# A float64 guard as a scale of ACT's absolute value, and squares, a division and copies moved from DVE to ACT and POOL, in attention followed by a squared-ReLU feed-forward layer

## The chip, the core and the metric

The kernel runs on one core of one Trainium2 chip. The metric is the device time of one execution in microseconds (us); lower is better. The core has a matrix engine (PE, with its weight loads PEld), a vector engine (DVE), an activation engine (ACT) and a general engine (POOL), each with its own queue of instructions that it works through in order. SP issues most DMAs, in order too, and ACT issues some. The engines and the DMAs wait for one another through semaphores.

## The reference

Two parts, one after the other. An attention between `x` (8 batches, 8 heads, 512 rows, 64 wide) and `state` (8, 8, 32, 64), read in both directions:

```python
scores = scale * np.matmul(x, state.transpose(0, 1, 3, 2))
a = np.exp(scores - scores.max(-1, keepdims=True)); a /= a.sum(-1, keepdims=True) + 1e-09
xread = np.matmul(a, state)
scores2 = scale * np.matmul(state, x.transpose(0, 1, 3, 2))
...
sread = np.matmul(a2, x)
return np.concatenate([xread, sread], axis=2).astype(np.float32)
```

Its output, 4352 rows of 512, goes through a feed-forward layer with a squared ReLU; `w_in` (512 x 2048) and `w_out` (2048 x 512) arrive as float64:

```python
h = x @ w_in
r = np.maximum(h, 0.0)
g = r * r
return (g @ w_out).astype(np.float32)
```

## The kernel before

**Exact halves.** A float32 factor is cut into two parts of a shorter format, `hi` and `lo`, by `split` (L96 to L98): ACT copies the value into the short format (L97), and the engine passed as `eng_lo` subtracts that from the value (L98). A product is then three matrix products.

**The weights.** They come as words of 64 bits, read as two 32-bit words. `singles` (L100 to L120) turns one 128x512 tile of them into float32: ACT takes the absolute value of the upper word (L107), DVE bounds it from below (L108), shifts and masks its bits (L109), puts the sign in (L113) and the topmost bits of the lower word (L117). Sixteen tiles of `w_in` (`w_raw` to `wf`, in `convert` of `z_part`) and sixteen of `w_out` (`wo_raw` to `wof`, in `wo_load`) go through it. The raw tiles share four buffers with other loads (tag `raw`); SP issues a load when a buffer is free, which is when L117 has read the tile in it.

**z.** The attention's first output times `w_in` is not formed from the output: for each batch the state is multiplied by `w_in` first. `z_part(G, k, g)` does this for a group `G` of four batches, 256 columns `k` of `w_in` and half of the heads `g`: load, `convert`, `cut` (a `split`, left out in the first six parts), and two products, whose result ACT copies out (`z_stage`, L215) and sends to DRAM (`zd`, L217). `z_fetch(b, k)` loads the batch's share of it back (`z_raw`, L230) and splits it into `z_hi` and `z_lo`. `z_state(0)` loads and splits the state for this (`stz_hi`, `stz_lo`, L141).

**The attention.** For a batch `b` and each half of the heads: `scores`, then `soft1` and `soft1b` (probabilities over the state, giving `a_hi` and `a_lo`), and, some batches later, `turn` (the other direction's probabilities `e2`, divided by their sum at L338 to L340, and transposed) and `read`.

**The feed-forward.** `mlp` takes a batch's 512 rows through columns `fc` of the hidden layer, 128 at a time. One such step is called a unit: `up` makes `ph` from z and a (six matmuls, L392), ReLU on ACT (L394), the square (on ACT for the first ten units, L396, on DVE for all others, L398) and a `split` into `g_hi` and `g_lo`; `down`, two units later, adds twelve matmuls (L418) into four banks `po`. At the end of a part, `rows` empties the four banks: with `move`, which takes DVE and ACT in turn, or with an addition on DVE (L599) where the sum exists already. The batches 0 and 1 are taken in two parts each (`BOTH`, L67: units 0 to 5 of batch 0, units 0 to 9 of batch 1, and then the rest of both), since the weights come in during that time; from batch 2 on a batch is one part of 16 units. After the eight batches a last pass of 16 units takes the rows of the state's direction.

**What sets the order.** The program is written in an order that two lists of steps with due times (`Ahead`, L475) interleave with the units. The scheduler behind the program then orders each engine's instructions anew by a timeline that it simulates, so a change in one instruction moves others.

Of the kernel before, what the change touches and what calls it, by code (L numbers as in the profile page):

```python
# [9 lines left out]
F32 = mybir.dt.float32  # L10
F32R = mybir.dt.float32r
I32 = mybir.dt.int32
AF = mybir.ActivationFunctionType
# [5 lines left out]
def memory_attention_then_relu2_ffn(  # L19
# [22 lines left out]
    nc = tc.nc  # L42
# [10 lines left out]
    NFC = DF // P  # L53
# [42 lines left out]
    def split(hi, lo, src, eng_lo):  # L96
        nc.scalar.copy(out=hi, in_=src)  # L97
        eng_lo.tensor_sub(out=lo, in0=src, in1=hi.bitcast(F32))  # L98

    def singles(out_f, words):  # L100

        low, high = words[..., 0], words[..., 1]
        bits = out_f.bitcast(I32)
        nc.scalar.activation(out_f, high.bitcast(F32), AF.Abs)  # L107
        nc.vector.tensor_scalar_max(out_f, out_f, 2.0**-15)  # L108
        nc.vector.tensor_scalar(  # L109
            out=bits, in0=bits, scalar1=3, scalar2=0x3FFFFFF8,  # L110
            op0=ALU.logical_shift_left, op1=ALU.bitwise_and,
        )
        nc.vector.scalar_tensor_tensor(  # L113
            out=bits, in0=high, scalar=-0x40000000, in1=bits,
            op0=ALU.bitwise_and, op1=ALU.bitwise_or,
        )
        nc.vector.scalar_tensor_tensor(  # L117
            out=bits, in0=low, scalar=29, in1=bits,
            op0=ALU.logical_shift_right, op1=ALU.bitwise_or,
        )  # L120


    def z_state(G):
        if G == 0:
            raw = sb.tile([P, H, GB * N], F32, name="st_f", tag="x_hl", bufs=1)
            st["raw"] = raw
        else:
            raw = sb.tile([P, H, GB * N], F32, name="st_raw", tag="raw", bufs=RAW)
        for j in range(2):
            nc.sync.dma_start(out=raw[j * D:(j + 1) * D].rearrange("d h m -> d (h m)"), in_=stT[G])  # L130
        hi = sb.tile([P, H, GB * N], F32R, name="stz_hi", bufs=1)
        lo = sb.tile([P, H, GB * N], F32R, name="stz_lo", bufs=1)
        if G:
            split(hi, lo, raw, nc.gpsimd)
        else:
            for i in range(2):
                own = slice(i * D, (i + 1) * D)
                other = slice((1 - i) * D, (2 - i) * D)
                for v in (hi, lo):
                    nc.gpsimd.memset(v[other, i::2, :].bitcast(F32), 0.0)  # L140
                split(hi[own, i::2, :], lo[own, i::2, :], raw[own, i::2, :], nc.vector)  # L141
        st[G] = hi, lo

    def z_part(G, k, g):
# [111 lines left out]
    def attention_group(b, g, pair):  # L256
# [79 lines left out]
        def turn():  # L336
            s2 = my["s2"]
            nc.vector.tensor_scalar_add(s2, s2, EPS)  # L338
            nc.vector.reciprocal(s2, s2)
            nc.vector.tensor_scalar_mul(my["e2"], my["e2"], s2)  # L340
            pt = ps_x.tile([P, NT, P], F32, name="pt", tag="px")
            for t in range(NT):
                nc.tensor.transpose(  # L343
                    out=pt[:, t, :], in_=my["e2"][:, t * P:(t + 1) * P], identity=ident
                )
            hl = sb.tile([P, NT, NQ, 2, 2 * N], F32R, name="e_hl", bufs=1)
            src = pt.rearrange("p t (q n) -> p t q n", n=2 * N)
            split(hl[:, :, :, 0, :], hl[:, :, :, 1, :], src, nc.vector)
            my["e"] = hl
# [31 lines left out]
    def mlp(width, fcs, first, rows, aux):  # L381
# [6 lines left out]
        def up(fc):  # L388
            ph = ps_h.tile([P, S], F32, name="ph", tag="ph")[:, :width]
            todo = first(fc)  # L390
            for i, (w, v) in enumerate(todo):
                nc.tensor.matmul(ph, lhsT=w, rhs=v, start=i == 0, stop=i == len(todo) - 1)  # L392
            r = sb.tile([P, S], F32, name="r", bufs=2)[:, :width]
            nc.scalar.activation(r, ph, AF.Relu)  # L394
            if units[0] < 10:
                nc.scalar.activation(ph, r, AF.Square)  # L396
            else:
                nc.vector.tensor_mul(out=ph, in0=ph, in1=r)  # L398
            units[0] += 1
            hi = sb.tile([P, S], F32R, name="g_hi", bufs=2)[:, :width]  # L400
            lo = sb.tile([P, S], F32R, name="g_lo", bufs=2)[:, :width]
            split(hi, lo, ph, nc.vector)
            gs[fc] = hi, lo
# [28 lines left out]

    units = [0]

    def move(t, dst, po):
        if t % 2:
            nc.scalar.copy(out=dst, in_=po)
        else:
            nc.vector.tensor_copy(out=dst, in_=po)
# [135 lines left out]
    for b, fcs in parts:  # L575
# [17 lines left out]
        def rows(t, po, b=b, fcs=fcs):  # L593
            if fcs[0] == 0:
                if t == 0:
                    sums[b] = sb.tile([P, NT, DM], F32, name="sum", bufs=2)
                move(t, sums[b][:, t, :], po)
            else:
                nc.vector.tensor_add(out=sums[b][:, t, :], in0=sums[b][:, t, :], in1=po)  # L599
            if fcs[-1] == NFC - 1:  # L600
                nc.sync.dma_start(
                    out=out[b * R + t * P:b * R + (t + 1) * P, :], in_=sums[b][:, t, :]
                )
# [74 lines left out]
```

## Time and profile before

| | |
|---|---|
| median of 3 runs | 716.35 us (716.26 to 717.2) |
| the profiled execution, its own time | 716.16 us |
| its span, first to last instruction | 714.4 us |
| PE, PEld busy | 669.0 us (94%), 550.3 us (77%) |
| DVE, ACT, POOL busy | 465.6 us (65%), 398.2 us (56%), 201.0 us (28%) |
| mean granted PE clock | 0.972 of full speed |
| moved by DMA | 90.58 MB |

"Busy" is the time in which an engine had at least one instruction in execution. The clock granted to PE is given as a share of full speed; at a lower one the same matmul takes longer. The views used further on are tables of busy time by stretches of the span (with the number of instructions, the granted clock, the share of the DMA engines' time in use and the rate), the chain of work that ended last, waits (who waited for whom: us in total, times, longest), groups of instructions with their mean duration, and timelines (start, duration). An engine starts an instruction before the one ahead of it has wholly finished, so the distance between two starts can be a little less than a duration.

### The profile page before, as it was taken

Reading aid. Unit: us, or ns where it says so; the run is one execution under the profiler, and the core shown is the slowest. Engines: PE = TensorE matmul, PEld = TensorE weight load, DVE = VectorE, ACT = ScalarE, POOL = GpSimd, SP = SyncE. Lnnn points to the kernel's source line nnn. Section 1 sums busy time; section 2 is a strip of 40 time slices with the busy share of each in tenths; the row PEclk is TensorE's granted clock in tenths of the full one; section 3 lists DMA queues with packets and bytes.
Section 4 is the critical chain, followed back from the end, with each engine's and each line's share of the span. In section 5 each row is a group of like instructions: output and inputs, shape, how many; then the busy total and the mean of one; then the engine's idle time right before and its main releaser. Section 6 shows DMA issues by size and latency. Waiting matters only on the chain.

```text
span 714.4 us, 9776 instructions
## 1 busy us (share of the span) xinstructions
PE 669.0 (94%) x3152; PEld 550.3 (77%) x3152; DVE 465.6 (65%) x789; ACT 398.2 (56%) x727; POOL 201.0 (28%) x181
## 2 busy tenths in 40 slices
PE   3579669999999999999999999999999999999997
PEld 1356457788888888888888878888888888888996
DVE  4969999949655964356955695697954445443453
ACT  3656676667654874367745564565564444442442
POOL 2412442335652460035302331325252022000000
PEclk9589879999999999999999999999999999999999
DMA  8787978733452552144333211322242112100321
GB/s 278 243 273 249 296 229 279 216 118 122 139 185 85 198 186 69 44 149 136 125 100 116 89 60 60 119 89 89 88 132 77 29 30 88 32 16 0 124 84 31
DMA packets 74548, 90.58 MB, mean 127 GB/s; under 512 B 7680, under 2 KB 57600, under 8 KB 74496
## 3 DMA queue, kind: packets, MB, share of 16 engines
q1 hardware_dynamic: 56896, 72.90, 32.5%
q10 hardware_dynamic: 17600, 17.04, 7.1%
q8 instruction: 25, 0.41, 0.2%
q14 instruction: 27, 0.22, 0.1%
HBM read 60.03 MB, written 29.88 MB: 126 GB/s over the span
## 4 chain that ended last, share of the span: by engine, by line
PE 76%; DVE 13%; DMA 7%; issue 2%; ACT 1%; SPq 1%; POOL 0%; DVEq 0%; ACTq 0%
PE po L418 45%; PE ph L392 24%; DMA wo_raw<-w_out 3%; PE pz L203 2%; PE pr L355 2%; DVE wof L113 1%; DMA z_raw<-zd 1%; PE pq L288 1%; DMA w_raw<-w_in 1%; DMA xt_raw<-xT 1%; PE pt L343 1%; DVE wof L117 1%; DVE wf L113 1%; DVE wof L109 1%; DVE wof L108 1%
## 5 line engine op out<-in xcount | busy, mean ns | idle before, releaser
L418 PE MATMUL po<-wo_hi,g_hi 128*128 128x512 f32 x544 | 216.3, 401 | 8.4 <-ACT g_hi L97 5.5
L418 PE MATMUL po<-wo_lo,g_hi 128*128 128x512 f32 x544 | 214.1, 395 | 0.0
L398 DVE TENSOR_TENSOR ph<-ph,r 128x512 f32<-128x512 f32 (+1 forms) x134 | 89.1, 665 | 171.5 <-ACT r L394 171.2
L394 ACT ACTIVATE r<-ph 128x512 f32<-128x512 f32 (+1 forms) x144 | 82.2, 572 | 174.2 <-PE ph L392 173.9
L418 PE MATMUL po<-wo_hi,g_lo 128*128 128x512 f32 x544 | 153.2, 393 | 0.2 <-DVE g_lo L98 0.2
L418 PEld LDWEIGHTS po<-wo_hi,g_hi 128*128 128x128 f32 x544 | 103.8, 191 | 31.1 <-ACT g_hi L97 7.1
L418 PEld LDWEIGHTS po<-wo_lo,g_hi 128*128 128x128 f32 x544 | 103.9, 191 | 19.6
L98 DVE TENSOR_TENSOR g_lo<-ph,g_hi 128x512 fp32r<-128x512 f32 (+1 forms) x144 | 94.4, 656 | 37.0 <-ACT g_hi L97 29.3
L418 PEld LDWEIGHTS po<-wo_hi,g_lo 128*128 128x128 f32 x544 | 102.1, 190 | 21.1 <-DVE g_lo L98 0.7
L97 ACT CAST g_hi<-ph 128x512 fp32r<-128x512 f32 (+1 forms) x144 | 80.8, 562 | 58.9 <-DVE ph L398 50.0
L392 PE MATMUL ph<-a_hi,z_hi 128*128 128x512 f32 x256 | 81.8, 402 | 2.2 <-ACT a_hi L97 1.2
L392 PE MATMUL ph<-a_hi,z_lo 128*128 128x512 f32 x256 | 79.7, 393 | 0.0
L392 PE MATMUL ph<-a_lo,z_hi 128*128 128x512 f32 x256 | 79.3, 390 | 0.0
L98 POOL TENSOR_TENSOR xn_hl<-xn_raw,xn_hl 128x1024 fp32r<-128x1024 f32 x16 | 38.9, 2431 | 138.1 <-ACT xn_hl L97 71.3
L182 POOL TENSOR_TENSOR w<-wf,w 64x512 fp32r<-64x512 f32 x32 | 43.0, 1343 | 71.2 <-ACT w L181 66.4
L392 PEld LDWEIGHTS ph<-a_hi,z_hi 128*128 128x128 f32 x256 | 47.2, 190 | 15.6 <-DVE g_lo L98 3.7
L392 PEld LDWEIGHTS ph<-a_hi,z_lo 128*128 128x128 f32 x256 | 48.2, 189 | 10.8 <-DVE z_lo L98 0.2
L392 PEld LDWEIGHTS ph<-a_lo,z_hi 128*128 128x128 f32 x256 | 47.9, 188 | 10.1
L98 POOL TENSOR_TENSOR xt_hl<-xt_raw,xt_hl 128x1024 fp32r<-128x1024 f32 x12 | 28.8, 2402 | 74.7 <-ACT xt_hl L97 37.0
L98 DVE TENSOR_TENSOR z_lo<-z_raw,z_hi 128x512 fp32r<-128x512 f32 x64 | 47.9, 749 | 0.0
L98 POOL TENSOR_TENSOR wo_lo<-wof,wo_hi 128x512 fp32r<-128x512 f32 x16 | 26.5, 1657 | 53.7 <-ACT wo_hi L97 53.7
L97 ACT CAST z_hi<-z_raw 128x512 fp32r<-128x512 f32 x64 | 39.4, 615 | 1.6 <-DMA z_raw<-zd 1.1
(99 smaller groups left out, 846.5 us busy)
## 6 DMA issues: line engine op xcount, KB each, us to landing
zd<-z_stage ACTq DMA_DIRECT2D x64, 256.0 KB, 2.8
z_raw<-zd SPq DMA_DIRECT2D x252, 64.0 KB, 2.4
xt_raw<-xT SPq DMA_DIRECT2D x16, 512.0 KB, 3.9
w_raw<-w_in SPq DMA_DIRECT2D x16, 512.0 KB, 5.1
wo_raw<-w_out SPq DMA_DIRECT2D x16, 512.0 KB, 4.8
xn_raw<-xn SPq DMA_DIRECT2D x16, 512.0 KB, 3.8
out<-sum SPq DMA_DIRECT2D x32, 256.0 KB, 2.5
wd<-wf SPq DMA_DIRECT2D x16, 256.0 KB, 3.1
```

The source lines that it names most:

```text
L97: nc.scalar.copy(out=hi, in_=src)
L98: eng_lo.tensor_sub(out=lo, in0=src, in1=hi.bitcast(F32))
L108: nc.vector.tensor_scalar_max(out_f, out_f, 2.0**-15)
L109: nc.vector.tensor_scalar(out=bits, in0=bits, scalar1=3, scalar2=0x3FFFFFF8, op0=ALU.logical_shift_left, op1=ALU.bitwise_and,)
L113: nc.vector.scalar_tensor_tensor(out=bits, in0=high, scalar=-0x40000000, in1=bits, op0=ALU.bitwise_and, op1=ALU.bitwise_or,)
L182: nc.gpsimd.tensor_sub(out=w[other], in0=wf[own], in1=w[own].bitcast(F32))
L203: nc.tensor.matmul(pz[:, q, :], lhsT=a[:, h, :], rhs=w, start=j == 0, stop=j == len(todo) - 1,)
L355: nc.tensor.matmul(pr[:, q].rearrange("p i c -> p (i c)"), lhsT=my["e"][:, t, q].rearrange("p i n -> p (i n)"), rhs=my["xn"][:, t, q].rear ...
L392: nc.tensor.matmul(ph, lhsT=w, rhs=v, start=i == 0, stop=i == len(todo) - 1)
L394: nc.scalar.activation(r, ph, AF.Relu)
L398: nc.vector.tensor_mul(out=ph, in0=ph, in1=r)
L418: nc.tensor.matmul(po[t], lhsT=g, rhs=w, start=i == 0 and j == 0, stop=i == last and j == 2)
```

## The change

The diff, with unchanged lines around it:

```diff
@@ singles
-        nc.scalar.activation(out_f, high.bitcast(F32), AF.Abs)
-        nc.vector.tensor_scalar_max(out_f, out_f, 2.0**-15)
+        nc.scalar.activation(out_f, high.bitcast(F32), AF.Abs, scale=2.0**-112)
         nc.vector.tensor_scalar(
-            out=bits, in0=bits, scalar1=3, scalar2=0x3FFFFFF8,
+            out=bits, in0=bits, scalar1=3, scalar2=0x7FFFFFF8,
             op0=ALU.logical_shift_left, op1=ALU.bitwise_and,
         )
         nc.vector.scalar_tensor_tensor(
-            out=bits, in0=high, scalar=-0x40000000, in1=bits,
+            out=bits, in0=high, scalar=-0x80000000, in1=bits,
@@ z_state
-                split(hi[own, i::2, :], lo[own, i::2, :], raw[own, i::2, :], nc.vector)
+                split(hi[own, i::2, :], lo[own, i::2, :], raw[own, i::2, :], nc.gpsimd)
@@ turn
-            nc.vector.tensor_scalar_mul(my["e2"], my["e2"], s2)
+            nc.scalar.mul(my["e2"], my["e2"], s2)
@@ up, in mlp
-            if units[0] < 10:
+            if units[0] < NFC:
                 nc.scalar.activation(ph, r, AF.Square)
             else:
                 nc.vector.tensor_mul(out=ph, in0=ph, in1=r)
@@
-    def move(t, dst, po):
-        if t % 2:
+    def move(t, dst, po, busy=False):
+        if t % 2 or busy:
             nc.scalar.copy(out=dst, in_=po)
         else:
             nc.vector.tensor_copy(out=dst, in_=po)
@@ rows
-                move(t, sums[b][:, t, :], po)
+                move(t, sums[b][:, t, :], po, b < 2)
```

Five edits. The scale 2^-112 puts a float64 exponent's upper bits, read as a float32's, where the shift by three needs them, and takes small ones to zero, so DVE's bound (32 instructions) is gone. Two subtractions of `stz_lo` go from DVE to POOL. Sixteen multiplications of `e2` go from DVE to ACT. The squares of units 10 to 15 go from DVE to ACT (`NFC` is 16). Four copies of `po` (banks 0 and 2 at the end of the first parts of batch 0 and of batch 1) go from DVE to ACT. In the changed kernel the absolute value stands on L108, since one line moved; L109 and all lines behind it are the same.

Three places where the order on an engine is another. The first is DVE's queue near its beginning, while the first two tiles of `w_in` are turned into float32. `wf_182` is the first tile and `wf_189` or `wf_188` the second; `pst` are the scores, `q1` their transpose, `nm2` and `m1` their maxima. Before, up to the first tile's last step; L108 of the first tile, L303 and L305 stand ahead of these rows:

```order
L109 TENSOR_SCALAR wf_182<-wf_182 128x512
L315 TENSOR_REDUCE m1_132<-q1_124 128x16
L108 TENSOR_SCALAR wf_189<-wf_189 128x512
L306 TENSOR_SCALAR nm2_126<-nm2_126 128x1
L113 SCALAR_TENSOR_TENSOR wf_182<-w_raw_117,wf_182 128x512
L98 TENSOR_TENSOR stz_lo_173<-st_f_169,stz_hi_172 64x4x128
L303 STREAM_TRANSPOSE q1_139<-pst_136 128x512
L305 TENSOR_REDUCE nm2_141<-pst_136 128x1
L98 TENSOR_TENSOR stz_lo_173<-st_f_169,stz_hi_172 64x4x128
L109 TENSOR_SCALAR wf_189<-wf_189 128x512
L117 SCALAR_TENSOR_TENSOR wf_182<-w_raw_117,wf_182 128x512
```

And after the change, from the queue's first row on:

```order
L109 TENSOR_SCALAR wf_182<-wf_182 128x512
L303 STREAM_TRANSPOSE q1_124<-pst_121 128x512
L305 TENSOR_REDUCE nm2_126<-pst_121 128x1
L113 SCALAR_TENSOR_TENSOR wf_182<-w_raw_117,wf_182 128x512
L315 TENSOR_REDUCE m1_132<-q1_124 128x16
L109 TENSOR_SCALAR wf_188<-wf_188 128x512
L306 TENSOR_SCALAR nm2_126<-nm2_126 128x1
L117 SCALAR_TENSOR_TENSOR wf_182<-w_raw_117,wf_182 128x512
```

L117 of the first tile is DVE's 14th instruction before and its 8th now; the second group's transposition and maximum, and both subtractions of `stz_lo`, no longer stand ahead of it.

The second is DVE's queue some twenty instructions later, at the fourth tile of `w_in` (`wf_272` before, `wf_268` now), the second half of the columns k = 1, from which unit 2's z is made. `wof_262` or `wof_259` is the first tile of `w_out`, `z_lo` belongs to unit 0. Before:

```order
L108 TENSOR_SCALAR wof_262<-wof_262 128x512
L109 TENSOR_SCALAR wof_262<-wof_262 128x512
L108 TENSOR_SCALAR wf_272<-wf_272 128x512
L113 SCALAR_TENSOR_TENSOR wof_262<-wo_raw_260,wof_262 128x512
L98 TENSOR_TENSOR z_lo_235<-z_raw_199,z_hi_234 128x512
L109 TENSOR_SCALAR wf_272<-wf_272 128x512
L117 SCALAR_TENSOR_TENSOR wof_262<-wo_raw_260,wof_262 128x512
L113 SCALAR_TENSOR_TENSOR wf_272<-w_raw_231,wf_272 128x512
L117 SCALAR_TENSOR_TENSOR wf_272<-w_raw_231,wf_272 128x512
```

And after the change:

```order
L109 TENSOR_SCALAR wf_268<-wf_268 128x512
L113 SCALAR_TENSOR_TENSOR wf_268<-w_raw_229,wf_268 128x512
L98 TENSOR_TENSOR z_lo_233<-z_raw_197,z_hi_232 128x512
L117 SCALAR_TENSOR_TENSOR wf_268<-w_raw_229,wf_268 128x512
L109 TENSOR_SCALAR wof_259<-wof_259 128x512
L113 SCALAR_TENSOR_TENSOR wof_259<-wo_raw_257,wof_259 128x512
L117 SCALAR_TENSOR_TENSOR wof_259<-wo_raw_257,wof_259 128x512
```

The tile of `w_in` is finished before the tile of `w_out` is begun; before, the two were interleaved and the tile of `w_out` came first.

The third is ACT's queue where the products of that fourth tile are copied out (`z_stage_368` and `z_stage_374` before, `z_stage_358` and `z_stage_364` now). `r` and `ph` belong to the units 0 and 1, `wof_283` and `wof_278` are the second tile of `w_out`. Before:

```order
L107 ACTIVATE wof_283<-wo_raw_281 128x512
L394 ACTIVATE r_244<-ph_233 128x512
L394 ACTIVATE r_327<-ph_320 128x512
L396 ACTIVATE ph_233<-r_244 128x512
L396 ACTIVATE ph_320<-r_327 128x512
L215 COPY z_stage_368<-pz_365 128x512
L97 CAST wo_hi0_268<-wof_283 128x512
L97 CAST g_hi_247<-ph_233 128x512
L97 CAST g_hi_330<-ph_320 128x512
L107 ACTIVATE wf_346<-w_raw_279 128x512
L215 COPY z_stage_374<-pz_371 128x512
```

And after the change:

```order
L394 ACTIVATE r_242<-ph_231 128x512
L108 ACTIVATE wof_278<-wo_raw_276 128x512
L396 ACTIVATE ph_231<-r_242 128x512
L394 ACTIVATE r_319<-ph_312 128x512
L97 CAST g_hi_245<-ph_231 128x512
L215 COPY z_stage_358<-pz_355 128x512
L396 ACTIVATE ph_312<-r_319 128x512
L108 ACTIVATE wf_338<-w_raw_274 128x512
L215 COPY z_stage_364<-pz_361 128x512
```

One ReLU stands ahead of the second tile of `w_out` now, and the second copy of z comes three instructions behind the first instead of five.

## The prediction

> **What bounds the kernel now.** I read the table of busy time by stretches first, since a mean over the span hides where time can be won. Its columns are PE, PEld, DVE, ACT and POOL busy (with counts), the granted PE clock, the DMA share and GB/s.
>
> ```profile
> 0.00:18.00 18.00, 6.63 (x12) 3.06 (x14) 8.82 (x17) 6.92 (x14) 4.96 (x13) 0.94 0.87 279
> 18.00:36.00 18.00, 10.38 (x42) 6.52 (x40) 17.73 (x34) 12.02 (x25) 7.57 (x6) 0.59 0.75 244
> 36.00:54.00 18.00, 13.47 (x43) 9.22 (x44) 11.10 (x21) 10.70 (x20) 2.56 (x2) 0.81 0.85 273
> 54.00:72.00 18.00, 16.35 (x72) 11.87 (x70) 17.40 (x33) 11.56 (x22) 4.82 (x3) 1.00 0.79 250
> 72.00:90.00 18.00, 11.56 (x46) 8.90 (x47) 17.62 (x31) 12.10 (x24) 8.46 (x7) 0.83 0.89 286
> 90.00:108.00 18.00, 11.37 (x52) 9.54 (x52) 17.76 (x31) 14.43 (x27) 7.40 (x4) 0.79 0.73 234
> 108.00:144.00 36.00, 34.78 (x160) 27.36 (x159) 35.06 (x54) 22.64 (x43) 12.25 (x8) 1.00 0.75 242
> 144.00:650.00 506.00, 505.19 (x2384) 421.38 (x2383) 312.13 (x519) 283.97 (x502) 152.95 (x141) 1.00 0.31 98
> ```
>
> Two regimes. From 144 us on PE is busy for 505.19 of 506 us at full clock: nothing done to DVE or ACT there can bring more than the missing 0.8 us. From 108 to 144 us 1.2 us are missing. Up to 108 us PE is busy for 69.76 of 108 (the sum of six rows), so 38 us are idle, and at clocks of 0.59 to 0.94 some of the busy time is lost too: 10.38 times 0.41, 13.47 times 0.19, 11.56 times 0.17, 11.37 times 0.21 and 6.63 times 0.06 make 11.6 us. Everything that the change can gain lies in these 50 us, and since PE is full afterwards, a microsecond saved there is a microsecond of the end.
>
> In four of those six stretches DVE is busy for 17.4 to 17.8 of 18 us; DMA's share is 0.73 to 0.89. The chain of work, asked for up to 108 us, and PE's waits, up to 108 us and then from there on, say how the two share the blame:
>
> ```profile
> by line: DMA wo_raw<-w_out 17.8%; DMA z_raw<-zd 8.4%; issue 8.1%; DMA w_raw<-w_in 7.2%; DMA xt_raw<-xT 6.5%; DVE wof L113 5.0%; DMA zd<-z_stage 4.6%; DVE wf L113 4.1%; DVE w L98 3.7%; DVE wof L117 3.5%; DVE wf L109 3.3%; DVE wf L117 3.3%; D
> ```
>
> ```profile
> PE pz L191 <- DVE wf L117: 7.2, 2, 5.2
> PE pz L191 <- DVE s L338: 6.7, 1, 6.7
> PE pz L191 <- ACT z_stage L215: 4.9, 2, 3.7
> ...
> PE po L418 <- ACT g_hi L97: 1.1, 2, 0.6
> PE ph L392 <- DVE g_lo L98: 0.8, 3, 0.3
> ```
>
> The DMA pieces named there are 44.5% of the chain (48 us), the rest is mostly DVE. So DVE is not alone: a load waits for a buffer that DVE has to free, and DVE waits for the load. A faster DVE shortens its own links and starts the loads sooner; it doesn't shorten a load. PE's largest early waits are for finished tiles of `w_in` (the row with L338 names the instruction right behind the tile's L117; it is the same wait) and for ACT's copies of z.
>
> **The change, part by part.** The bound on DVE (L108), 24 of the 32 before 108 us:
>
> ```profile
> 0.00:54.00 54.00, 5.63 (x11) 0.78 0.82 265
> 54.00:108.00 54.00, 9.28 (x13) 0.87 0.81 257
> ...
> L108 DVE TENSOR_SCALAR wf<-wf x16: 357/419/1482, 9.1 to 119.0; 128x512 f32<-128x512 f32 x16
> L108 DVE TENSOR_SCALAR wof<-wof x16: 409/426/1521, 28.2 to 138.2; 128x512 f32<-128x512 f32 x16
> ```
>
> 5.63 and 9.28 us of DVE's time (the DVE column of the first two rows, of L108 alone; then minimum, median and maximum in ns). On the chain up to 108 us L108 has 12 pieces of 6.47 us in all, the first and the last of which, with the two long ones, are these; the multiplication by L340 has 3 pieces of 1.74 us and the copies into `sum` 2 of 0.64 us, of which the longest are shown:
>
> ```profile
> 23.98 0.29 DVE wf L108
> 33.94 1.49 DVE wf L108
> 94.25 1.45 DVE wof L108
> 100.04 0.34 DVE wof L108
> 22.29 0.87 DVE e L340
> 91.66 0.57 DVE sum L439
> ```
>
> *Up to unit 2 (54 us).* The order moves work as well. The first z product waits for L117 of the first tile:
>
> ```profile
> 9.12 0.43 DVE L108 TENSOR_SCALAR wf<-wf 128x512 f32<-128x512 f32 x1 [9.12 <-ACT wf L107]
> 13.38 0.67 DVE L98 TENSOR_TENSOR stz_lo<-st_f,stz_hi 64x512 fp32r<-64x512 f32 x1
> 16.35 0.69 DVE L117 SCALAR_TENSOR_TENSOR wf<-w_raw,wf 128x512 int32<-128x512 int32 x1
> ```
>
> From 13.38 to 16.35 DVE does what now stands elsewhere (two `stz_lo`, L303, L305, the second tile's L109): 2.97 us. Two L108 go too, about 0.34 each from start to start, and L109 of the second tile comes ahead at about the same: the tile is ready 3.3 us sooner. For the fourth tile two L340 (0.40 and 0.87 on the chain) and three L108 (0.29, 0.35, 0.42) go away, and the first tile of `w_out` is no longer interleaved, whose L113 alone is this:
>
> ```profile
> 29.45 1.68 DVE wof L113
> ```
>
> With L109 and L117 of that tile (0.3 and 0.6) it is 2.6 us. Together 3.3 + 1.3 + 1.1 + 2.6 = 8.3 us for the fourth tile. Not all of it reaches unit 2: its z goes through ACT's copies, and there the queue is in order.
>
> ```profile
> 36.11 0.67 ACT L107 ACTIVATE wof<-wo_raw 128x512 f32<-128x512 f32 x1 [1.73 <-DMA wo_raw<-w_out]
> 38.67 0.59 ACT L215 COPY z_stage<-pz 128x512 f32<-128x512 f32 x1
> ```
>
> ACT stood at the second tile of `w_out` for 1.73 us, with that copy queued behind it, and still does: only one ReLU has passed it. That load starts sooner by what the fourth tile frees sooner, less what the DMA takes longer. Below stands the chain's own sum up to 54 us, 2.90 + 0.43 (L108) + 1.27 (L340) = 4.6; above 8.3. I take 6, a little under the middle.
>
> *From 54 to 108 us.* DVE saturated. The chain's pieces there: L108 3.14, L340 0.47, `sum` 0.64, together 4.25 us. Lower end: L108's long pieces last 1.45 instead of 0.34, in the time of a POOL subtraction; POOL's work stays, so that wait may fall to the next DVE instruction; less 1.1, that makes 3.1. Upper end: DVE is the sole bound and all that leaves it here counts, 9.28 of L108 and 1.1 on the chain of the other two, 10.4 us. I take 4.3.
>
> The Trainium skill, GPSIMD Engine Reference, section Key points, states that POOL shares its SBUF interfaces with VectorE and contends with DVE instructions in a two-port mode or with two SBUF inputs. By that rule the waits in the long pieces (1.49 and 1.45, less 0.34 each) stay on the chain under another name, and the sum below would be 9.0 in place of 11.3: 707, inside the forecast's own range. The maximum of 1482 ns against a median of 419 agrees with contention; that the wait moves, no run here shows yet.
>
> *Squares, and 108 us on.* Five of the six moved squares lie between 108 and 144 us, one behind. They relieve DVE where PE lacks 1.2 us. I take 1.0; zero is as possible.
>
> *What is added.* ACT gets, before 108 us, four products and two copies, about 0.6 each by ACT's squares, 3.6 us:
>
> ```profile
> L396 ACT ACTIVATE ph<-r 128x512 f32<-128x512 f32 x10 | 5.9, 599 | 0.1
> L317 ACT ACTIVATE q<-q 128x512 f32<-128x512 f32 x16 | 10.1, 628 | 0.7 <-DVE q L316 0.7
> L107 ACT ACTIVATE wf<-w_raw 128x512 f32<-128x512 f32 x16 | 10.7, 672 | 15.8 <-DMA w_raw<-w_in 9.3 <-PE pz L191 3.3 <-DVE w L98 3.2
> L182 POOL TENSOR_TENSOR w<-wf,w 64x512 fp32r<-64x512 f32 x32 | 43.0, 1343 | 71.2 <-ACT w L181 66.4
> ```
>
> It was busy for 67.7 of 108 us (the sum of its column), so idle time covers them; without that cover they cost at most 3.6 us, in ReLU and copies queued behind. POOL gets two subtractions of 64x512, 1.34 each by the last row, ahead of the first probabilities; DVE's sums of those come behind the first two tiles now, so I cost them at nothing, 2.7 if that cover is gone. The scale in ACT's absolute value is no step of its own: the exponential `q` has a scale and takes 628 ns, the absolute value without one 672, so between 32 times 44 ns less and nothing; I take nothing. The other twelve products by the sums, behind 144 us, go from an idle DVE to an idle ACT beside a full PE: nothing.
>
> Sum: 6 + 4.3 + 1.0 = 11.3 us. 716.16 (the profiled execution; its span and 1.76 around it) less 11.3 is 704.9; the median of the runs is 0.2 above that execution. **Forecast: 705 us.** Its own range is 700 to 709.
>
> **The rivals.**
>
> *DMA takes DVE's place.*
>
> ```profile
> DMA packets 16273, 28.20 MB, mean 261 GB/s; under 512 B 1571, under 2 KB 9772, under 8 KB 16266
> ```
>
> These 28.2 MB fell in the first 108 us. At the best stretch's 286 GB/s they take 98.6 us, which allows 9.4; at the mean of 261 nothing. If loads get slower as they crowd, of the early part only the first tile's 3.3 us stay, and about 1 later: 4 us, 712 us. For it: 0.73 to 0.89 used already, and the tallest pieces of the chain are loads. Against it: 286 GB/s at a share of 0.89 makes 321 at a full one, so room is there, and gaps come from buffers freed late.
>
> *All of it counts.* If loads follow at once, 8.3 + 10.4 + 1.2 make 19.9 us: 696. For it: DVE's 17.7 of 18. Against: 48 us of loads on the chain.
>
> *Slower: ACT held by loads, with PE's work queued behind.* ACT meets each raw tile first, in order.
>
> ```profile
> ACT wf L107 <- DMA w_raw<-w_in: 6.7, 4, 3.8
> ACT wof L107 <- DMA wo_raw<-w_out: 5.3, 5, 1.7
> ```
>
> Nine of 24 tiles hold it for 12.0 us, 1.33 each. With DVE faster, more tiles find their load still on its way; each holds squares, ReLUs and `g_hi`, on which PE waits. All 15 others would cost 20 us, less 11.3 makes 725; it decides from the ninth on (9 times 1.33 is 12). I price it at 13 of them: 722. Against it: an earlier free buffer starts that load earlier too, so the wait is bounded by the load, not added to it.
>
> *The change does nothing.* The new order wastes what DVE is spared: 716.2.
>
> **How the numbers follow.** Forecast 0.52, DMA 0.22, all of it 0.16, slower 0.06, nothing 0.04. Two in ten may be left out: 695 to 713 holds the forecast, the DMA case at its price and nearly all of the large one. A change under 0.2% (1.4 us) can't be told from none. Faster: 0.52 + 0.22 + 0.16 = 0.90; same 0.04; slower 0.06.
>
> **What would show it.** The places to look at are the first z product and unit 2's first `ph`:
>
> ```profile
> 17.09 2.09 PE L191 MATMUL pz<-wf,st_f 64*128 64x256 f32 x8 [6.66 <-DVE s L338]
> ...
> 54.05 1.48 PE L392 MATMUL ph<-a_hi,z_hi 128*128 128x512 f32 x4
> ```
>
> They should start near 13.8 and 48 us, and PE should be full from about 97 instead of 108 us. DVE should fall below 17 of 18 us in the stretches from 54 us on; if it does while PE still waits and the DMA share nears 0.9 and more, the DMA case holds. If long DVE pieces of 1.4 us remain in number, now on L109 and L113, the waits beside POOL moved. If ACT's waits for `w_raw` and `wo_raw` exceed 24 us, the slow case is at work. What would make me wrong most simply is a PE that is not full behind 144 us.

## The result, and the profile after

| | median | runs | ratio to the kernel before, run beside it |
|---|---|---|---|
| before | 717.02 us (716.26 to 720.27) | 9 | |
| changed | 714.23 us (711.8 to 715.23) | 9 | 0.995, 95% interval 0.9935 to 0.9965 |

The change makes the kernel faster by 2.8 us by the medians (0.995 of 717 us is 3.6 less, with an interval of 2.5 to 4.7), where 11.3 were forecast; 714.2 lies outside the range. The profiled execution of the changed kernel took 714.7 us, with a span of 712.8.

The table of busy time by stretches of the changed kernel, columns as before (PE, PEld, DVE, ACT, POOL busy, with counts; granted PE clock; DMA share; GB/s), with one stretch more at the end:

```profile
0.00:18.00 18.00, 8.17 (x20) 4.13 (x22) 9.11 (x18) 8.48 (x19) 9.43 (x16) 0.94 0.90 297
18.00:36.00 18.00, 8.04 (x34) 5.14 (x31) 14.54 (x26) 13.24 (x27) 6.80 (x5) 0.68 0.88 278
36.00:54.00 18.00, 17.01 (x41) 10.77 (x42) 9.76 (x15) 9.03 (x17) 2.72 (x2) 0.62 0.86 271
54.00:72.00 18.00, 14.66 (x67) 10.76 (x66) 17.95 (x31) 13.21 (x26) 7.33 (x5) 1.00 0.85 259
72.00:90.00 18.00, 12.36 (x59) 9.96 (x58) 17.84 (x28) 14.47 (x28) 9.40 (x7) 0.91 0.81 250
90.00:108.00 18.00, 15.02 (x67) 12.58 (x66) 16.37 (x27) 14.48 (x28) 3.61 (x3) 0.81 1.02 340
108.00:144.00 36.00, 36.00 (x172) 30.24 (x172) 26.28 (x35) 25.35 (x47) 9.91 (x7) 1.00 0.68 205
144.00:650.00 506.00, 501.89 (x2359) 418.64 (x2359) 309.79 (x501) 289.38 (x513) 152.57 (x140) 1.00 0.31 96
200.00:250.00 50.00, 46.81 (x217) 39.06 (x216) 36.13 (x57) 32.87 (x61) 21.57 (x17) 0.97 0.47 148
```

That last stretch in the kernel before:

```profile
200.00:250.00 50.00, 49.70 (x240) 41.53 (x239) 36.00 (x62) 33.17 (x62) 19.40 (x16) 1.00 0.48 158
```

Read each row as a loss: idle PE (the stretch less PE's busy time), and busy time times one less the clock. Summed so:

| loss in us | before | changed | forecast gain | gain shown |
|---|---|---|---|---|
| 0 to 54 | 23.5 idle + 7.2 clock | 20.8 + 9.5 | 6 | 0.4 |
| 54 to 108 | 14.7 + 4.4 | 12.0 + 4.0 | 4.3 | 3.1 |
| 108 to 144 | 1.2 | 0 | 1.0 | 1.2 |
| 144 to 650 | 0.8 | 4.1 + 1.4 | 0 | -4.7 |

The gains of this one pair of profiles sum to nothing, where the spans differ by 1.6 us: the table is rough, since the clock is given in hundredths and half a hundredth of 500 us is 2.5 us. DVE is spared as meant (26.28 instead of 35.06 us in the stretch from 108 on), and PE is full there. Two things are not as forecast: the front (the time up to 144 us) gains less, and PE is not full behind 144 us, where nearly all of the new loss lies between 200 and 250. PE's waits behind 144 us name it; before, none was longer than 0.5 us:

```profile
PE ph L392 <- DVE nm L306: 3.2, 1, 3.2
```

The timeline of the changed kernel around that wait (start, duration, engine, line, operation; the bracket is the idle time before):

```profile
231.82 0.72 ACT L340 ACTIVATE e<-e,s 128x512 f32<-128x512 f32 x1 [0.16 <-DVE s L339]
...
232.63 0.61 PE L392 MATMUL ph<-a_hi,z_hi 128*128 128x512 f32 x2
...
232.92 1.05 ACT L97 CAST xn_hl<-xn_raw 128x1024 fp32r<-128x1024 f32 x1
...
234.10 2.40 POOL L98 TENSOR_TENSOR xn_hl<-xn_raw,xn_hl 128x1024 fp32r<-128x1024 f32 x1 [3.66 <-ACT xn_hl L97]
234.25 2.29 DVE L323 TENSOR_SCALAR s<-s 128x16 f32<-128x16 f32 x1
...
236.45 0.70 DVE L303 STREAM_TRANSPOSE q<-st 128x512 f32<-128x512 f32 x1
...
237.37 2.62 POOL L182 TENSOR_TENSOR w<-wf,w 64x512 fp32r<-64x512 f32 x2 [0.87 <-ACT w L181]
...
237.80 2.34 DVE L98 TENSOR_TENSOR sp_hl<-sp_raw,sp_hl 64x128 fp32r<-64x128 f32 x2
...
240.77 0.68 DVE L98 TENSOR_TENSOR g_lo<-ph,g_hi 128x512 fp32r<-128x512 f32 x1
...
241.51 1.22 PE L392 MATMUL ph<-a_hi,z_hi 128*128 128x512 f32 x2 [3.19 <-DVE nm L306]
```

And the same place of the program before (L323 starts 7.0 us later there):

```profile
238.67 1.05 ACT L97 CAST xn_hl<-xn_raw 128x1024 fp32r<-128x1024 f32 x1
...
238.87 0.48 DVE L340 TENSOR_SCALAR e<-e,s 128x512 f32<-128x512 f32 x1
...
239.85 2.41 POOL L98 TENSOR_TENSOR xn_hl<-xn_raw,xn_hl 128x1024 fp32r<-128x1024 f32 x1 [2.78 <-ACT xn_hl L97]
...
241.28 1.01 DVE L323 TENSOR_SCALAR s<-s 128x16 f32<-128x16 f32 x1
242.21 0.59 DVE L98 TENSOR_TENSOR sp_hl<-sp_raw,sp_hl 64x128 fp32r<-64x128 f32 x2
...
243.42 2.64 POOL L182 TENSOR_TENSOR w<-wf,w 64x512 fp32r<-64x512 f32 x2 [1.15 <-ACT w L181]
244.04 0.68 DVE L98 TENSOR_TENSOR g_lo<-ph,g_hi 128x512 fp32r<-128x512 f32 x1
```

L323 has 16 columns and lasts 2.29 us: it starts 0.15 us behind POOL's subtraction and ends with it (236.50). The two subtractions of `sp_hl` start 0.43 us behind POOL's next pair and end 0.15 us after it. Before, L323 met only the last microsecond of POOL's piece, and `sp_hl` fell into the gap between two. The row after both in DVE's queue that matters is `g_lo`: it reads the `ph` bank that PE needs for the next unit (the wait is listed under L306, which stands just behind it). PE stood for 3.19 us and then worked at half clock: two matmuls of L392 take 1.22 us, where two took 0.61 at 232.63. What moved is ACT: the product of `e2` (L340) now stands there ahead of the cast of `xn_hl` and no longer on DVE, so POOL's subtraction starts 0.15 us ahead of L323 instead of 1.43. The order on DVE differs a little too: two further instructions, L324 and L315, 0.76 us from start to start, stand ahead of `g_lo` now and stood behind it before.

### The profile page after: what moved, and what is told of

It reads as the page before. It is cut to its first block, busy times and chain, and to the rows that moved or that the text cites. A ratio compares the mean times of both kernels' runs of the same rounds, so it can differ in the third digit from the quotient of the medians.

```text
span 712.8 us, 9732 instructions
## 1 busy us (share of the span) xinstructions
PE 670.9 (94%) x3152; PEld 553.4 (78%) x3152; DVE 449.2 (63%) x729; ACT 411.1 (58%) x753; POOL 201.8 (28%) x183
## 4 chain that ended last, share of the span: by engine, by line
PE 82%; DVE 7%; DMA 5%; ACT 3%; issue 1%; SPq 0%; POOL 0%; ACTq 0%; DVEq 0%; POOLq 0%
PE po L418 48%; PE ph L392 26%; PE pz L203 2%; PE pr L355 2%; PE pq L288 1%; DVE sp_hl L98 1%; DMA st_f<-stT 1%; PE pz L191 1%; DMA w_raw<-w_in 1%; PE pt L343 1%; DMA xt_raw<-xT 1%; DMA wo_raw<-w_out 1%; ACT z_stage L215 1%; DMA wd<-wf 1%; DVE st L294 1%
## 5 line engine op out<-in xcount | busy, mean ns | idle before, releaser
L398 DVE TENSOR_TENSOR ph<-ph,r 128x512 f32<-128x512 f32 (+1 forms) x128 | 84.9, 663 | 172.2 <-ACT r L394 172.1
L392 PE MATMUL ph<-a_hi,z_hi 128*128 128x512 f32 x256 | 81.3, 400 | 3.6 <-DVE nm L306 3.2
L392 PE MATMUL ph<-a_hi,z_lo 128*128 128x512 f32 x256 | 79.7, 392 | 1.6 <-DVE z_lo L98 1.6
L392 PE MATMUL ph<-a_lo,z_hi 128*128 128x512 f32 x256 | 79.6, 391 | 0.0
L392 PEld LDWEIGHTS ph<-a_hi,z_hi 128*128 128x128 f32 x256 | 47.5, 191 | 14.6 <-DVE nm L306 3.4
L392 PEld LDWEIGHTS ph<-a_hi,z_lo 128*128 128x128 f32 x256 | 48.4, 189 | 12.6 <-DVE z_lo L98 2.1
L392 PEld LDWEIGHTS ph<-a_lo,z_hi 128*128 128x128 f32 x256 | 48.3, 189 | 10.3
L98 DVE TENSOR_TENSOR z_lo<-z_raw,z_hi 128x512 fp32r<-128x512 f32 x64 | 51.9, 811 | 2.7 <-ACT z_hi L97 2.6
L98 POOL TENSOR_TENSOR xt_hl<-xt_raw,xt_hl 128x1024 fp32r<-128x1024 f32 x12 | 29.6, 2466 | 55.4 <-ACT xt_hl L97 45.0
L215 ACT COPY z_stage<-pz 128x512 f32<-128x512 f32 x64 | 37.7, 589 | 8.3 <-PE pz L191 5.3
```

Of the source, the lines that this page charges most:

```text
L215: nc.scalar.copy(out=stage, in_=pz)
```

## The experiments

Each kernel ran in turn with the kernel before on the same chip; the medians of that were 717.1 to 717.5 us throughout.

**One part of the change undone.** Two theories: the *collision* just shown, caused by `e2` on ACT; and a *squeeze*, by which DVE has too little room between 225 and 250 us, so that any gain is lost there again. Edits against the changed kernel:

```diff
# no_e2 (turn)
-            nc.scalar.mul(my["e2"], my["e2"], s2)
+            nc.vector.tensor_scalar_mul(my["e2"], my["e2"], s2)
# no_sq (up)
-            if units[0] < NFC:
+            if units[0] < 10:
# no_stz (z_state)
-                split(hi[own, i::2, :], lo[own, i::2, :], raw[own, i::2, :], nc.gpsimd)
+                split(hi[own, i::2, :], lo[own, i::2, :], raw[own, i::2, :], nc.vector)
# guard_only: these three, and (rows)
-                move(t, sums[b][:, t, :], po, b < 2)
+                move(t, sums[b][:, t, :], po)
```

> The change with one part undone: the product of e2 and its sum's inverse stays on DVE (L340). The collision theory: in the changed kernel a lead of 7 us at unit 32 falls to 2 to 3 us by unit 40, because e2's product on ACT delays the cast of xn_hl behind it by 0.7 us, so that POOL's 2.4 us subtraction of xn_hl falls on DVE's L323 (2.29 us instead of 1.01) and the next one on sp_hl (2.34 instead of 0.59); PE waits 3.2 us and then runs 3.4 us at half clock. With e2 back on DVE the lead of 6 to 7 us should stay past unit 40, no PE wait over 1 us between 200 and 260 us, time 708 to 711. The squeeze theory: from 225 to 250 us DVE has as much to do as time, so whatever the front wins is taken back there in any order: PE waits 3 to 5 us there again, time 713 to 715.

> Only the scale in ACT's absolute value, the other four parts undone: 32 L108 leave DVE and nothing is moved. If the guard is nearly all of the front's gain, unit 16 comes 5 to 7 us sooner than before. Collision theory: no e2 on ACT, so nothing is given back near 238 us, time 709 to 712. Squeeze theory: given back near 238 us, time 713 to 716.

> The change with the squares of the units 10 to 15 back on DVE. PE is full in both kernels while these units run, so both theories expect no difference to the changed kernel, 713 to 715.5, with the wait near 238 us still there. If the squares mattered, unit 16 would come over 1 us later.

> The change with the two subtractions of stz_lo back on DVE. The first tile of w_in is then ready some 1 us later (two times 0.6 us on DVE, if they stand ahead of it), and POOL does not hold DVE's L113 of the second tile for 0.9 us. Both theories: 713.5 to 716 with the wait near 238 us; if POOL's work in the front was what cost the missing 4 us there (11 expected, 7 seen), the front gains and unit 16 comes over 1.5 us sooner than in the changed kernel.

| kernel | us | ratio, 95% interval |
|---|---|---|
| no_e2 | 708.28 | 0.9883, 0.9858 to 0.9909 |
| guard_only | 707.61 | 0.9869, 0.9852 to 0.9886 |
| no_sq | 709.44 | 0.99, 0.9883 to 0.9916 |
| no_stz | 711.2 | 0.9915, 0.9897 to 0.9932 |

The squeeze falls: `no_e2` and `guard_only` are ahead of the kernel before at 225 us and stay ahead. The scale alone gives 9.6 us, more than the collision theory expected; the four moved parts together take most of it back. But the first form of the collision theory falls too: `no_sq` and `no_stz` have `e2` on ACT and no wait over 0.4 us near 240 us; both theories had expected 713 us or more of them. In `no_sq` DVE's queue reads:

```profile
241.91 0.67 DVE L98 TENSOR_TENSOR g_lo<-ph,g_hi 128x512 fp32r<-128x512 f32 x1
...
244.00 3.75 DVE L98 TENSOR_TENSOR sp_hl<-sp_raw,sp_hl 64x128 fp32r<-64x128 f32 x2
```

`sp_hl` is stretched even more, 3.75 us, but `g_lo` stands ahead of it. So the wait needs two things: a stretched instruction, and behind it in DVE's queue one that PE waits for. That is "collision and queue" below. `no_stz` stays 1.8 us or more behind the other three; its six runs have the lowest mean clock (0.968 to 0.971, the others 0.972 to 0.983), and why is not shown.

**The collision taken away, all else kept.** `late_e2`, `sp_pool` and `no_mv` each have one line other than the changed kernel. `late_e2` puts two of the sixteen products back on DVE; `sp_pool` gives two subtractions of `sp_hl` to POOL, where they can't collide with it. `after_again` is the changed kernel unaltered, `no_mv` has the four copies of `po` back on DVE.

```diff
# late_e2 (turn)
-            nc.scalar.mul(my["e2"], my["e2"], s2)
+            (nc.vector.tensor_scalar_mul if b == 3 else nc.scalar.mul)(my["e2"], my["e2"], s2)
# sp_pool (pad)
-                split(sp_hl[rows, :, :, 0, at], sp_hl[rows, :, :, 1, at], raw[rows], nc.vector)
+                split(sp_hl[rows, :, :, 0, at], sp_hl[rows, :, :, 1, at], raw[rows], nc.vector if b != 4 else nc.gpsimd)
```

> The changed kernel with one line other: the two products of e2 that belong to batch 3 (at 231.8 and 245.8 us) stand on DVE again, all others stay on ACT. The queues of DVE (266 rows) and PE (716 rows) are the same as in the changed kernel up to about 231 us. Theory 'collision and queue' (POOL's subtraction for xn_hl falls on L323 and the next one on sp_hl, 2.29 and 2.34 us instead of 1.01 and 0.60, with g_lo queued behind on DVE): without the product on ACT the cast of xn_hl comes 0.6 us sooner and POOL's subtraction with it, so L323 lasts 1.0 to 1.6, sp_hl 0.6 to 1.2, PE's wait near 240 us falls from 3.19 to under 1.0 us and the half clock behind it goes; 714.2 less 3.2 less 1.5 makes 709.5, range 708.5 to 711.5. Rival 'queue alone' (g_lo is placed too late on DVE, whatever POOL does): here too L303 and L305 and both sp_hl stand ahead of g_lo, so the wait stays above 2.5 us; 713 to 715.

> The changed kernel with one line other: the two subtractions of sp_hl for batch 4 (64x128 each) go from DVE to POOL. DVE's queue is the same as in the changed kernel for 273 rows, then lacks these two, with L315 and g_lo next as before. Theory 'collision and queue': L323 is still stretched by POOL's subtraction of xn_hl (2 to 2.4 us), but the 2.34 us of sp_hl are gone from in front of g_lo, so PE's wait near 240 us falls from 3.19 to about 0.9; 714.2 less 2.3 makes 711.9, and 710.4 if the half clock behind the wait goes too; range 709.5 to 712.5. Rival 'queue alone': two uncontended sp_hl are worth 0.6 us, the wait stays above 2.4; 713.5 to 714.5.

> The changed kernel with the four copies of po (banks 0 and 2 at the end of the first parts of batches 0 and 1) back on DVE. It completes the set of kernels with one part undone. Theory 'collision and queue': in DVE's queue g_lo now stands ahead of L294, L303, L305 and sp_hl, so however long these get PE doesn't wait for them: no wait over 1.5 us between 200 and 260 us, and a time of 708 to 711.5 like the other three. Theory 'each moved part is worth what DVE is spared': four copies of 0.64 us, at most two of them on the chain, so 714.2 plus 0.6 to 1.3, 714.8 to 715.5.

> The changed kernel itself, a second time, beside the others. If the collision belongs to the program (queues and durations) and not to one execution: L323 again over 2 us, sp_hl over 2 us, a wait of PE of 2.5 to 3.5 us near 240 us, and 712 to 715. If it belongs to one execution: no such wait and 707 to 711.

| kernel | us | ratio, 95% interval |
|---|---|---|
| late_e2 | 708.91 | 0.9885, 0.9865 to 0.9905 |
| sp_pool | 708.44 | 0.9886, 0.9863 to 0.9909 |
| no_mv | 707.46 | 0.9863, 0.9841 to 0.9884 |
| after_again | 712.96 | 0.9938, 0.9917 to 0.996 |

The timeline of `late_e2`: POOL's piece starts 1.43 us ahead of L323 again, as before the change, and `sp_hl` fits the gap. L324 and L315 stand behind `g_lo` again too.

```profile
230.25 2.42 POOL L98 TENSOR_TENSOR xn_hl<-xn_raw,xn_hl 128x1024 fp32r<-128x1024 f32 x1 [2.77 <-ACT xn_hl L97]
...
231.68 1.02 DVE L323 TENSOR_SCALAR s<-s 128x16 f32<-128x16 f32 x1
232.62 0.59 DVE L98 TENSOR_TENSOR sp_hl<-sp_raw,sp_hl 64x128 fp32r<-64x128 f32 x2
...
234.44 0.68 DVE L98 TENSOR_TENSOR g_lo<-ph,g_hi 128x512 fp32r<-128x512 f32 x1
```

PE's longest wait there is 0.3 us. In `sp_pool` L323 still collides and L324 and L315 still stand ahead of `g_lo`, but `sp_hl` is gone from DVE, and the wait is a quarter of what it was:

```profile
229.54 2.29 DVE L323 TENSOR_SCALAR s<-s 128x16 f32<-128x16 f32 x1
...
233.64 0.67 DVE L98 TENSOR_TENSOR g_lo<-ph,g_hi 128x512 fp32r<-128x512 f32 x1
```

```profile
PE ph L392 <- DVE nm L306: 0.8, 1, 0.8
```

'Queue alone' expected waits above 2.4 us in both, so it falls; so does, with `no_mv`, the theory that each part undone costs what DVE was spared (714.8 to 715.5 expected; 707.46 is a little below the other theory's range as well). The second execution of the changed kernel shows the collision to the hundredth: the program has it, not one run.

```profile
233.83 2.28 DVE L323 TENSOR_SCALAR s<-s 128x16 f32<-128x16 f32 x1
...
237.37 2.34 DVE L98 TENSOR_TENSOR sp_hl<-sp_raw,sp_hl 64x128 fp32r<-64x128 f32 x2
```

By the ratios of `late_e2` and of the two measurements of the changed kernel the collision costs 0.53% to 0.65% of 717 us, 3.8 to 4.7 us, where each ratio is uncertain by about 0.2%; the profile shows 3.2 of waiting and 1.4 of half clock. `sp_pool` came out 2 to 3.5 us lower than its point of 711.9 or 710.4; that surplus is not explained (its six executions had a mean clock of 0.978 to 0.985, those of the changed kernel in the first table 0.971 to 0.979). `late_e2` meets another stretched `sp_hl` at 450 us, with the square L398 behind it, on which `g_hi` and PE wait; no run takes this one away:

```profile
450.87 2.71 DVE L98 TENSOR_TENSOR sp_hl<-sp_raw,sp_hl 64x128 fp32r<-64x128 f32 x2
...
455.40 0.69 DVE L398 TENSOR_TENSOR ph<-ph,r 128x512 f32<-128x512 f32 x1
```

```profile
456.76 0.50 PE L418 MATMUL po<-wo_hi,g_hi 128*128 128x512 f32 x1 [1.73 <-ACT g_hi L97]
```

**One part alone, added to the scale.** The edits are those of the diff, each on top of `guard_only`; `guard_sq_mv` has the squares and the copies. `early_e2` is the changed kernel with the products of the batches 0 and 1 on DVE.

> The kernel before with the scale and the products of e2 on ACT; squares, stz_lo and copies as before. With the scale alone the time was 707.6. Theory 'collision and queue': here sp_hl stands behind g_lo of the unit that PE needs next, so the collision costs PE nothing: no wait over 1.5 us between 200 and 260 us. The four early products (0.72 us each on ACT against 0.47 on DVE, near 20 to 70 us) stand in front of the weights' absolute values: 0 to 1.2 us of loss. 707.0 to 709.5. Theory 'e2 on ACT is the harmful part': the loss of the changed kernel comes back without the other three parts; 711 to 715.

> The kernel before with the scale, and the two subtractions of stz_lo on POOL; all else as before. With the scale alone: 707.6. The prediction's own term: 2.97 us of DVE's work leave the first tile's way, the first z product starts that much sooner, so 707.6 less 3.0 makes 704.6 (range 703.5 to 705.5). Theory 'DVE is not what ends last there any more': the first product starts near 12.5 us instead of 15 to 16, but the following ones wait for the loads of the next tiles as before: 706.5 to 709.

> The kernel before with the scale, and the squares of units 10 to 15 on ACT. With the scale alone: 707.6, with PE full from 108 us on. The prediction's own term: 1.0 less, 706.6. Theory 'DVE is not what ends last there any more': nothing to gain where PE is full, 707 to 709, the upper part of it by squares of 0.6 us that stand on ACT in front of the weights' absolute values.

> The kernel before with the scale, and the four copies of po on ACT. With the scale alone: 707.6. The prediction's own term: 0.64 less, 707.0. Theory 'DVE is not what ends last there any more': 707 to 709; the change without this part took 707.5, so it may cost 1 to 2 us: a copy on ACT stands between the copies of z.

> The kernel before with the scale, the squares of units 10 to 15 and the four copies on ACT; stz_lo and e2 stay on DVE. Singly they gave 1.0 and 1.4 less than the scale alone (707.6). If the parts add up: 705.2, range 704.4 to 706. If each re-ordering of the queues brings a gain or a loss of its own (as the three parts sq, mv and stz together took 708.3 although singly they sum to 705.1): 706.5 to 709.

> The changed kernel with the four products of e2 of the batches 0 and 1 (at 20 to 70 us) back on DVE; those of the batches 2 to 7 stay on ACT. Here sp_hl stands between two sums, with g_lo of a unit queued behind. If the late products on ACT do the harm wherever such a queue is met: a wait of 1 us or more near 215 to 250 us, 711 to 714. If the early ones do it, by 0.72 us each on ACT where DVE took 0.47: no wait over 0.8 us between 200 and 260 us, and a loss before 108 us of 40 to 42 us as with all products on DVE; 707 to 709.

| kernel | us | ratio, 95% interval |
|---|---|---|
| guard_e2 | 709.65 | 0.9896, 0.9876 to 0.9916 |
| guard_stz | 707.48 | 0.987, 0.9849 to 0.9892 |
| guard_sq | 706.64 | 0.9852, 0.9831 to 0.9873 |
| guard_mv | 706.21 | 0.9856, 0.983 to 0.9881 |
| guard_sq_mv | 706.64 | 0.9841, 0.9818 to 0.9864 |
| early_e2 | 710.11 | 0.9887, 0.9865 to 0.9909 |

Against `guard_only` (0.9869) none of the first five is clear of the intervals; `guard_e2` comes nearest. What the medians suggest is that squares and copies bring about a microsecond (their own terms, 1.0 and 0.64), that `stz_lo` brings nothing where 3.0 were expected, and that `e2` costs two. Whether squares and copies add up is open: by the medians the two together are no better than either, but by the ratios, which set each kernel against the one before on its own chip, they bring 0.17% and 0.13% singly and 0.28% together. `early_e2` (710.1) fits neither of its theories: no wait over 0.3 us between 200 and 260 us, but one of 1.72 us for `g_hi` at 459 us, and a loss before 108 us of 45, not 40 to 42. Whether the early products on ACT do harm by themselves stays open. `guard_only`, `guard_stz`, `guard_sq`, `guard_mv`, `guard_sq_mv` and `no_mv` beat both kernels of the diff; between 706.2 and 707.6 the runs can't rank them.

**Is DVE still the bound in the front?** `no_sign` leaves the sign of the weights out (L113 gone, so that products are formed with absolute values), on top of `guard_only`.

```diff
-        nc.vector.scalar_tensor_tensor(
-            out=bits, in0=high, scalar=-0x80000000, in1=bits,
-            op0=ALU.bitwise_and, op1=ALU.bitwise_or,
-        )
```

> The kernel before with the scale alone, and with the sign of the weights left out (no L113), so products are formed with absolute values. DVE is spared 32 instructions, 19.0 us of them before 108 us in the kernel with the scale (11.5 and 7.5); the bound that the scale took away was 14.9 us there and brought 9.6. Theory 'DVE still bounds the front': in the same proportion 12 us, 694 to 698. Theory 'loads and ACT's queue bound the front now': under 4 us, 703.5 to 707.

696.54 us, ratio 0.9708 (0.9688 to 0.9729): 11 us less than `guard_only` for 19.0 us of DVE's work before 108 us. So DVE still bounds the front, and the share of its work that counts, 0.58, is near that of the scale (9.6 for 14.9, 0.64). The case in which loads take DVE's place has not come, though it is near: over the first 108 us `guard_only` moved 293 GB/s at a DMA share of 0.87, this one 315 at a share of 0.96.

```profile
0.00:108.00 108.00, 78.14 (x295) 55.90 (x296) 88.06 (x151) 73.59 (x141) 37.62 (x35) 0.83 0.87 293
```

```profile
0.00:108.00 108.00, 85.06 (x353) 62.80 (x354) 83.13 (x138) 80.20 (x155) 39.21 (x38) 0.89 0.96 315
```

## Why the prediction was wrong, step by step

**The step that failed** is the last of the parts: that the other twelve products, behind 144 us, "go from an idle DVE to an idle ACT beside a full PE: nothing". DVE's mean share and PE's full stretch were read as cover. But DVE's queue is in order, and one of its instructions can last as long as the POOL instruction that it meets. The product on ACT shifted that meeting by 1.28 us (from 1.43 to 0.15 us behind POOL's start), in front of a `g_lo`. That costs 3.8 to 4.7 us in this kernel; in `no_e2` and `guard_only` no wait behind 144 us is over 0.8 us. `late_e2` and `early_e2` have a wait of 1.7 us at another turn. Without those 3.8 to 4.7 us the time would be 709.5 to 710.4, inside 695 to 713. The text named this opening itself: what would make it wrong most simply is "a PE that is not full behind 144 us". The rest of the 8.5 us that are missing is missing from the front.

**Up to unit 2, 6 us: too high by 3 us or more.** The first tile came sooner, as worked out: the first z product starts at 12.49 us instead of 17.09 (forecast 13.8), though in the second execution of the changed kernel only at 15.55. Unit 2 did not: 54.93, not 48. It is a fair mark, since 96 matmuls stand ahead of it in both kernels. In the changed kernel PE's rows are:

```profile
12.49 1.51 PE L191 MATMUL pz<-wf,st_f 64*128 64x256 f32 x8 [1.85 <-DVE wf L117]
...
25.82 2.08 PE L191 MATMUL pz<-wf,st_f 64*128 64x256 f32 x8 [6.66 <-ACT wf L108]
...
54.93 1.49 PE L392 MATMUL ph<-a_hi,z_hi 128*128 128x512 f32 x4
```

The chain of work that ended last passes here through pieces that the change moved:

```profile
12.22 1.29 POOL stz_lo L98
...
13.52 1.05 POOL q L316
...
20.19 1.31 ACT e L340 x2
...
29.61 5.16 DMA wo_raw<-w_out
```

And on ACT, where the copies of z queue:

```profile
34.80 0.66 ACT L108 ACTIVATE wof<-wo_raw 128x512 f32<-128x512 f32 x1 [2.69 <-DMA wo_raw<-w_out]
```

The lead of the first tile is lost at the third (6.66 us of idle PE). ACT takes the absolute value of that tile at 21.40 us, without waiting for its load: ACT's rows show no pause over 0.15 us from 14.60 on, and two products of `e2` stand right ahead of it. That run of ACT's work begins behind `stz_lo` and L316 on POOL. Both moves had been put at nothing ("idle time covers them" on ACT; on POOL "2.7 if that cover is gone"). Later ACT stands 2.69 us at the second tile of `w_out` instead of 1.73, and from 37 to 51 us the chain is PE itself, at half clock until 50.0. `guard_stz` moves `stz_lo` alone: its first and third products start at 13.05 and 24.29 us, in `guard_only` at 14.39 and 25.64, but its time is the same. So the 2.97 us of `stz_lo`'s move, half of the term, are worth about nothing; where that lead goes, no run shows.

How much the whole front gains, one profile can't say. The changed kernel, `late_e2` and `sp_pool` have the same instructions in the same order on every engine up to 231 us, so four executions can be compared there. The first matmul of a unit starts at, in us:

| | unit 2 | unit 16 | unit 40 |
|---|---|---|---|
| before | 54.05 | 149.83 | 263.78 |
| changed | 54.93 | 142.70 | 261.92 |
| changed, second execution | 53.31 | 142.27 | 261.68 |
| `late_e2` | 52.29 | 139.72 | 254.16 |
| `sp_pool` | 51.09 | 137.99 | 253.83 |

At unit 2 they are between 0.9 us late and 3.0 ahead, where 6 were forecast. At unit 16 they are 7.1 to 11.8 us ahead, where the three terms of the front make 11.3 (445 matmuls stand ahead of it instead of 449). Between the two marks they gain 6.8 to 8.9 us, where 5.3 were forecast. So one term was too high and the others too low, and that the sum of the three came near is in part luck. From unit 16 to unit 40 the changed kernel loses 5.3 and 5.5 us of its lead, `sp_pool` 1.9 and `late_e2` 0.5 (1004 matmuls stand ahead of unit 40 in the changed kernel and in `sp_pool`, 1000 in `late_e2`): the collision once more. By medians the front gains 7.5 to 10 us of the 11.3: 2.8 and the 4.7 lost behind 144 us for the changed kernel, 8.4 and 1.7 for `late_e2`.

**From 54 to 108 us, 4.3 us.** 3.1 by the table. The doubt at this place was right for `w_in`: stalls beside POOL stay on DVE under another name. The groups of instructions up to 108 us, before:

```profile
L113 DVE SCALAR_TENSOR_TENSOR wf<-w_raw,wf 128x512 int32<-128x512 int32 x13 | 10.6, 818 | 0.1
L117 DVE SCALAR_TENSOR_TENSOR wf<-w_raw,wf 128x512 int32<-128x512 int32 x13 | 9.7, 744 | 0.1
...
L108 DVE TENSOR_SCALAR wf<-wf 128x512 f32<-128x512 f32 x14 | 8.3, 594 | 14.0 <-ACT wf L107 14.0
```

and in the changed kernel:

```profile
L113 DVE SCALAR_TENSOR_TENSOR wf<-w_raw,wf 128x512 int32<-128x512 int32 x15 | 14.7, 982 | 0.3
L117 DVE SCALAR_TENSOR_TENSOR wf<-w_raw,wf 128x512 int32<-128x512 int32 x15 | 14.0, 935 | 0.1
```

A tile of `w_in` is spared 594 ns and pays 164 and 191 ns of it back in the two instructions that follow; L109 takes 46 less. For `w_out` nothing is paid back in all: by the same view the four instructions of a tile took 3024 ns before, and the three left take 2352. The Trainium skill, GPSIMD Engine Reference, section Key points, has POOL contend with DVE instructions in a two-port mode or with two SBUF inputs, and the rows of `w_in` agree with that. The forecast weighed such contention for the front alone, and it decided the time at 240 us.

There L323 ends with POOL's piece, whether it started 0.15 us (2.29) or 1.43 us (1.02) behind it. The Trainium skill, SBUF — State Buffer, section Who interferes with whom, says it as a rule for a DVE instruction in a two-port mode or with two SBUF inputs: whichever of the two starts first keeps the shared ports for its whole instruction, and the other stands still. The rows of L323 agree with that; in which mode it works, no run here shows.

**The squares, 1.0.** The number came near (1.2 by the table, 1.0 by the median of `guard_sq`, within its interval), but its reason isn't shown: in `guard_only` PE is full from 108 to 144 us without the moved squares (36.00 of 36 us). **The scale as no step of its own**: right; ACT's absolute values take 679 and 688 ns on average (`w_in`, `w_out`), before 670 and 675. DVE's bound, which it replaces, held 6.47 us of the chain, and taking it away alone brought 9.6, the only part of the change whose gain is clear of noise. **ACT held by loads**: its waits for `w_raw` and `wo_raw` are 6.1 and 2.7 us, before 6.7 and 5.3; the price of 722 did not come. **DMA in DVE's place**: as the bound of the whole front refuted by `no_sign`, which moved 315 GB/s where the case allowed 286.

**The range and the chances.** Faster at 0.90 was right. The range's upper end, 713, came from the cases of the front alone; no rival priced a stall where PE was full.

## What to carry to other kernels

Moving an instruction from one idle engine to another, in a stretch where the matrix engine is full, was not free here. It shifted when two other engines met; look in each queue for the instruction that the matrix engine waits for, and count what may be stretched ahead of it. Take such a change apart before judging it: here one of five edits was the gain, and another, in the order that the five together made, lost nearly half of it again. Where the clock varies, compare fronts by medians of many runs: with the same queues unit 16 started at 137.99 to 142.70 us, more than most of the edits are worth.

## What the runs showed of the hardware

- A DVE instruction of 16 columns (L323) takes 0.16 us alone (`no_mv`, 237.24 us) and 2.29 us beside a POOL subtraction of 2.40 us. A transposition of 128x512 keeps its usual length beside POOL (L303, 0.69 us at 450.44 in the changed kernel, inside a POOL subtraction of 1.36 from 450.31), and so does the subtraction `g_lo`, one of whose inputs is the PSUM tile `ph` (0.68 us at 244.04 before, inside POOL's pair of 2.64 from 243.42).
- The half clock comes and goes in steps of 3.41 us, on a grid that stands differently to the start in each execution: the granted clock was half from 15.9 to 29.6 and 36.4 to 50.0 us in the changed kernel, from 13.5 to 34.0 and 54.5 to 57.9 in its second profile. The queues are the same, and the loss to the clock before 54 us was 9.5 us in the one and 5.3 in the other, with 20.8 and 22.7 us idle.
- 3.19 us of idle PE at 238 us were followed by one such step of half clock (241.2 to 244.6); the waits of 1.7 us at 456 us (`late_e2`) and 459 us (`early_e2`) were not.
